# Splitting the first query load of an attention lead-in, with four fewer idle transposes

## The chip, the cores and the metric

The kernel runs on one NeuronCore of a Trainium2 chip. The metric is the device time of one execution in microseconds (us); the number compared is the median over runs.

## The reference

The computation is a thresholded attention followed by a two-layer MLP with a hard-swish gate. B = 8 batches, H = 8 heads, S = 576 tokens, D = 64, all float32.

```python
scores = (q @ k.T) / sqrt(D)
scores = where(scores >= max(scores) - tau, scores, -1e9)
attn = softmax(scores)                      # sum + 1e-9 in the denominator
x = (attn @ v) as [B*S, H*D]                # 4608 x 512
h = x @ w_in                                # 512 -> 2048
out = (h * clip(h + 3, 0, 6) / 6) @ w_out   # 2048 -> 512
```

## The kernel before

Heads are handled four at a time, a "quad" (16 quads in all, two per batch), and within a quad as two pairs of heads. A pair's queries and keys must stand with the head dimension on the partitions before their product can be formed, so each pair's blocks are transposed once: on TensorE (PE) for the first two batches, on VectorE (DVE) later. A quad gives nine "slots": eight of 128 queries by 576 keys for two heads, and one for the remaining 64 tokens of all four heads. The 144 slots run one after the other in an order written out by hand: in slot n the kernel computes the row maxima of slot n+1 (L302, DVE), mask and exponential (L309, L314, ScalarE, here ACT), normalisation (L322, GpSimd, here POOL), the scores of slot n+2 (L287, PE), and in the gaps the products with v and the MLP's matmuls.

The change is in the lead-in, the stretch ahead of slot 0. There is no scheduler: every engine executes its instructions in the order in which the program lists them, and a transfer starts in the order in which its queue's engine issues it. The names in it:

- `load_quad(0)` puts five load jobs in a list, and all are started at once: keys of pair 0 (`load_k(0)`, tile `km`, two transfers of 128 KB, one per head), queries of pair 0 (`load_q(0)`, tile `nq`, two of 128 KB), the last 64 tokens of keys and queries (`rest`, tiles `kr` and `nq`, four of 32 KB), and keys and queries of pair 1. All are issued by SyncE (SP), except the queries of pair 0, which ACT issues. A partition's piece of any of these loads is runs of 64 floats, 256 bytes each. For queries, tile t holds tokens 128t to 128t + 127; for keys a partition holds four successive tokens.
- `warm_up(17)` (L185) issues 17 transposes of a 128x128 float32 identity into a PSUM bank that nobody reads. They depend on the identity alone.
- Then the real transposes, in this order on PE: four of the keys (L232), `warm_up(4)`, the first 128 tokens of the queries (L456), the rest of the keys (L457), three more query tiles (L459), three more idle transposes (L461), and the scores of slots 0 and 1 (L287).
- The evictions from PSUM: ACT copies the main keys (L222) and half of the rest of the keys (L465); DVE copies the first queries (L464), the other half of the rest of the keys (L466), and the other queries (L467).
- After that, `warm_up(8)` in slot 0 and `warm_up(6)` in slots 0 to 7 put further idle transposes behind the scores.

```python
    load_quad(0)
    start(loads, 5)
    ...
    warm_up(17)
    ...
    evict = transpose_k(0)
    warm_up(4)
    nc.tensor.transpose(lead[:, 0, 0:P], q_main[:, 0, 0:2, :], identf[:])   # L456
    nc.tensor.transpose(lead[:, 1, 0:P], nat[0][2][:], identf[:])           # L457
    for t in range(1, 4):
        nc.tensor.transpose(q_rows[:, t * P:(t + 1) * P], q_main[:, t, 0:2, :], identf[:])  # L459
```

Transfers signal one of eight semaphores in turn; a ninth transfer uses the first one again and waits for its earlier transfer.

Of the kernel before, what the change touches and what calls it, by code (L numbers as in the profile page):

```python
# [15 lines left out]
P = 128  # L16
# [4 lines left out]
def kernel(  # L21
# [10 lines left out]
    nc = tc.nc  # L32
# [8 lines left out]
    NB = 2  # L41
# [40 lines left out]
    def load_quad(quad):  # L82
        b, g = divmod(quad, 2)
        nat[quad] = (nat_pool.tile([P, 1152], F32, tag="nq", name="nq"),
                     nat_pool.tile([P, 4, 4, D], F32, tag="km", name="km"),
                     nat_pool.tile([P, 2 * D], F32, tag="kr", name="kr"))
        nq, km, kr = nat[quad]

        def main(dst, src, h, order, by=nc.sync):
            by.dma_start(out=dst[:, :, h, :], in_=src[b, 4 * g + h, 0:512, :].rearrange(order, t=4))  # L90

        def blocks_q(n, a, j):
            c = 32 * (2 * a + j)
            nc.sync.dma_start(out=nq[c:c + 32, n * S:(n + 1) * S].rearrange("p (k d) -> p k d", d=32),
                              in_=q[b, 4 * g + 2 * n + a, :, 32 * j:32 * j + 32].rearrange("(k r) d -> r k d", r=32))

        def blocks_k(n, a, j):
            c = 32 * (2 * a + j)
            nc.sync.dma_start(
                out=km[c:c + 32].rearrange("p t h d -> p (t h d)")[:, n * 512:(n + 1) * 512].rearrange(  # L100
                    "p (t m d) -> p t m d", t=4, d=32),
                in_=k[b, 4 * g + 2 * n + a, 0:512, 32 * j:32 * j + 32].rearrange("(m r t) d -> r t m d", r=32, t=4))

        def load_k(n):
            if b < NB:
                for a in range(2):
                    main(km, k, 2 * n + a, "(p t) d -> p t d")
            else:
                for a in range(2):
                    for j in range(2):  # L110
                        blocks_k(n, a, j)

        def load_q(n):
            if b < NB:
                for a in range(2):
                    main(nq[:, 0:1024].rearrange("p (t h d) -> p t h d", h=4, t=4), q, 2 * n + a, "(t p) d -> p t d",
                         by=nc.scalar if quad == n == 0 else nc.sync)
            else:
                for a in range(2):
                    for j in range(2):  # L120
                        blocks_q(n, a, j)

        def rest():
            for dst, src in ((kr[:], k), (nq[:, 1024:1152], q))[0:2 if b < NB else 1]:
                for n in range(2):
                    (nc.sync if b < NB else nc.gpsimd).dma_start(out=dst[64 * n:64 * n + 64, :].rearrange("p (h d) -> p h d", h=2),
                                      in_=src[b, 4 * g + 2 * n:4 * g + 2 * n + 2, 512:S, :].rearrange("h p d -> p h d"))

        def both():
            rest()  # L130
            load_k(1)

        if b < NB:
            loads.extend((lambda: load_k(0), lambda: load_q(0), rest, lambda: load_k(1), lambda: load_q(1)))
        else:
            loads.extend((lambda: load_q(0), lambda: load_k(0), lambda: load_q(1), both))
# [46 lines left out]
    def warm_up(count):  # L183
        for _ in range(count):
            nc.tensor.transpose(ps[:, HB, 0:P], identf[:], identf[:])  # L185

    warm_up(17)
    identb = singles.tile([P, P], BF16)
    nc.vector.tensor_copy(out=identb[:], in_=identf[:])
    three = singles.tile([P, 1], F32)  # L190
# [181 lines left out]
    def mm1(item, hb=HB):  # L372
        b, ni, c0 = item
        if c0 is None:
            for ki in range(KI):
                nc.tensor.matmul(ps[:, hb, :], xR[b // 2][:, ki, :], w_in_sb[:, ki, ni * P:ni * P + 512],  # L376
                                 start=(ki == 0), stop=(ki == KI - 1))
        else:
            for n in range(2):
                for ki in range(KI):  # L380
                    nc.tensor.matmul(ps[:, hb, n * 256:(n + 1) * 256], w_in_sb[:, ki, (ni + n) * P:(ni + n + 1) * P],  # L381
                                     xT[b][:, ki, c0:c0 + 256], start=(ki == 0), stop=(ki == KI - 1))
        return ps[:, hb, :]
# [134 lines left out]
    for n, sl in enumerate(queue):  # L518
        quad, slot = sl.quad, sl.slot
        b, g = divmod(quad, 2)  # L520
# [25 lines left out]
        if todo1:  # L546
            item, then = todo1.pop(0)
            h = mm1(item, OB if n > N1 and n % 2 and not pieces else HB)
# [149 lines left out]
```

## Time and profile before

| | |
|---|---|
| median of 4 runs | 522.12 us (521.65 to 523.26) |
| profiled execution, its time | 521.65 us |
| its span, first to last instruction | 519.9 us |
| PE busy | 502.9 us, 97% |
| DVE, ACT, POOL busy | 442.3, 451.9, 299.3 us |
| lead-in, up to the first scores matmul | 7.03 us |

Times inside the profile count from the span's start. "L232" is line 232 of the kernel before. In the timeline a row gives the start, the length, the engine, the line and operation, the tiles written and read, and how many instructions were merged; square brackets give the idle time before it and what ended it. "SPq" and "ACTq" rows are transfers being issued, "PEld" is the weight load of a matmul. A PE record is longer than the distance to the next one because matmuls are pipelined, so rates are read from distances or from a stretch divided by its count.

### The profile page before, as it was taken

The numbers are of one execution on the slowest core, as the hardware profiler recorded it, in microseconds if no ns is written. First come the engines' busy times: TensorE is split into PE (matmuls) and PEld (weight loads), VectorE is DVE, ScalarE is ACT, GpSimd is POOL, SyncE is SP. The second block draws the span as 40 slices with busy tenths as digits, with TensorE's granted clock in tenths as the row PEclk, the third lists the DMA queues.
The fourth block names the chain that finished last, engine by engine and source line by source line (L and its number), as shares of the span: only waits on it lengthen the run. The fifth ranks groups of instructions, "written<-read, shape, count | busy, mean of one in ns | idle before, by whom it ended". The sixth has DMA issues, their size and how long they took to land.

```text
span 519.9 us, 12068 instructions
## 1 busy us (share of the span) xinstructions
PE 502.9 (97%) x4089; PEld 321.1 (62%) x4145; DVE 442.3 (85%) x1124; ACT 451.9 (87%) x980; POOL 299.3 (58%) x538
## 2 busy tenths in 40 slices
PE   8999999999999999999999999999999999999997
PEld 6765556666665666666655666666655666667463
DVE  3788888998999999999999999999999999878151
ACT  3999979999999999999999999999999999995060
POOL 1788869756676666657566656657566755551000
PEclk9999999999999999999999999999999999999999
DMA  5899999989999899999999999999999996564222
GB/s 131 125 173 156 153 152 136 203 140 177 166 175 165 157 174 154 193 160 180 163 168 179 173 175 160 178 161 178 161 172 162 177 170 113 112 113 70 83 61 61
DMA packets 314094, 78.77 MB, mean 152 GB/s; under 512 B 296624, under 2 KB 309168, under 8 KB 314032
## 3 DMA queue, kind: packets, MB, share of 16 engines
q1 hardware_dynamic: 294464, 67.90, 77.3%
q0 software_dynamic: 18368, 9.71, 15.0%
q8 instruction: 32, 0.52, 0.4%
q10 hardware_dynamic: 1200, 0.39, 0.3%
q14 instruction: 30, 0.25, 0.2%
HBM read 36.70 MB, written 9.44 MB: 89 GB/s over the span
## 4 chain that ended last, share of the span: by engine, by line
PE 77%; ACT 3%; DVE 2%; issue 2%; DMA 1%; POOL 0%; POOLq 0%; DVEq 0%
PE ps L287 24%; PE ps L415 23%; PE ps L381 19%; PE ps L346 6%; PE ps L376 2%; ACT s L309 1%; PE ps L349 1%; ACT s L314 1%; DMA pR<-pn 1%; ACT r L389 1%; DMA g<-go 1%; DVE s L302 1%; DVE g L404 1%; POOL pn L322 0%; PE ps L257 0%
## 5 line engine op out<-in xcount | busy, mean ns | idle before, releaser
L322 POOL TENSOR_SCALAR pn<-s,rinv 128x576 bf16<-128x576 f32 x288 | 210.6, 743 | 19.5 <-issue 4.4
L302 DVE TENSOR_SCALAR_CACHE_REDUCE s<-ps 128x576 f32<-128x576 f32 x288 | 205.0, 748 | 17.6 <-PE ps L287 9.0
L309 ACT ACTIVATE s<-s,bias 128x576 f32<-128x576 f32 x288 | 205.9, 763 | 6.0 <-POOL bias L305 5.7
L314 ACT ACTIVATE s<-s 128x576 f32<-128x576 f32 x288 | 192.5, 671 | 0.3
L287 PE MATMUL ps<-kT,qT 64*128 64x384 f32 (+7 forms) x1280 | 174.0, 419 | 4.7 <-DVE s L302 3.8
L287 PEld LDWEIGHTS ps<-kT,qT 64*128 64x128 f32 (+1 forms) x1280 | 103.6, 175 | 59.3 <-issue 15.8
L381 PE MATMUL ps<-xT,w_in_sb 128*128 128x256 bf16 x1024 | 130.8, 273 | 1.3 <-DVE g L404 0.7
L415 PE MATMUL ps<-w_out_sb,g 128*128 128x512 bf16 x524 | 123.4, 379 | 2.8 <-issue 0.2
L381 PEld LDWEIGHTS <-w_in_sb 128*128 128x128 bf16 x1024 | 95.5, 98 | 41.0 <-issue 22.1
L305 POOL TENSOR_SCALAR bias<-m 128x2 f32<-128x2 f32 x144 | 26.9, 187 | 154.1 <-DVE rinv L317 135.6
L404 DVE SCALAR_TENSOR_TENSOR g<-r,ps 128x512 bf16<-128x512 f32 x128 | 87.6, 686 | 9.5 <-ACT r L389 5.5
L415 PEld LDWEIGHTS <-g 128*128 128x128 bf16 x576 | 56.3, 98 | 56.7
L389 ACT ACTIVATE r<-ps,three 128x512 f32<-128x512 f32 x81 | 55.4, 687 | 28.9 <-PE ps L381 21.3
L314 ACT ACTIVATION_READ_ACCUMULATOR s<-s 128x1 f32 x288 | 54.5, 189 | 0.0
L391 DVE TENSOR_SCALAR r<-ps 128x512 f32<-128x512 f32 x63 | 42.9, 680 | 0.0
L346 PE MATMUL ps<-pT,vm 128*64 128x256 bf16 (+1 forms) x480 | 39.1, 285 | 0.0
L346 PEld LDWEIGHTS <-vm 128*64 128x64 bf16 x736 | 27.2, 110 | 16.6 <-issue 15.4
L357 DVE CAST xT<-ps 128x256 bf16<-128x256 f32 (+1 forms) x60 | 26.2, 437 | 12.8 <-PE ps L349 12.8
L423 DVE TENSOR_SCALAR osb<-ps 128x512 f32<-128x512 f32 x31 | 20.9, 673 | 13.3 <-PE ps L415 13.3
L302 DVE DVE_READ_ACCUMULATOR s<-ps 128x1 f32 x288 | 23.8, 83 | 0.0
L317 DVE RECIPROCAL rinv<-rsum 128x2 f32<-128x2 f32 x144 | 23.0, 160 | 0.6 <-ACT s L314 0.6
L143 POOL DMA_DIRECT2D vm<-in_v_dram x28 | 21.4, 766 | 0.7 <-issue 0.7
(57 smaller groups left out, 259.1 us busy)
## 6 DMA issues: line engine op xcount, KB each, us to landing
out_dram<-osb SPq DMA_DIRECT2D x31, 256.0 KB, 2.8
nq<-in_q_dram SPq DMA_DIRECT2D x96, 72.0 KB, 3.4
km<-in_k_dram SPq DMA_DIRECT2D x96, 64.0 KB, 3.1
vm<-in_v_dram POOLq DMA_DIRECT2D x24, 128.0 KB, 4.0
km<-in_k_dram SPq DMA_DIRECT2D x16, 128.0 KB, 3.7
w_in_sb<-in_moe_w_in_dram POOLq DMA_DIRECT2D x16, 128.0 KB, 3.7
w_out_sb<-in_moe_w_out_dram POOLq DMA_DIRECT2D x16, 128.0 KB, 4.8
pT<-pn SPq DMA_TRANSPOSE x117, 4.0
```

Source lines behind the costliest of these rows:

```text
L287: nc.tensor.matmul(ps_flat[rows, c0:c0 + w], qT_of(pair)[a * 64:(a + 1) * 64, q0:q0 + rows.stop - rows.start], kT_of(pair)[a * 64:(a + 1) ...
L302: nc.vector.tensor_scalar(out=sl.s[:, i, :], in0=ps_flat[:, c0:c0 + S], scalar1=1.0, scalar2=None, op0=Alu.mult, op1=Alu.max, accum_out=sl ...
L305: nc.gpsimd.tensor_scalar(out=sl.bias[:], in0=sl.m[:], scalar1=-scale, scalar2=tau, op0=Alu.mult, op1=Alu.add)
L309: nc.scalar.activation(out=s, in_=s, func=Act.Prelu, bias=sl.bias[:, i:i + 1], scale=scale, alpha=REJECT)
L314: nc.scalar.activation(out=s, in_=s, func=Act.Exp, accum_out=sl.rsum[:, i:i + 1])
L322: nc.gpsimd.tensor_scalar(out=pn[:, i, :], in0=sl.s[:, i, :], scalar1=sl.rinv[:, i:i + 1], scalar2=1.0, op0=Alu.mult, op1=Alu.mult)
L346: nc.tensor.matmul(pb[a * 64:(a + 1) * 64, :], vm[:, 2 * hp + a, c * D:(c + 1) * D], pT[:, 5 * a + c, cols], start=(c == 0), stop=False)
L381: nc.tensor.matmul(ps[:, hb, n * 256:(n + 1) * 256], w_in_sb[:, ki, (ni + n) * P:(ni + n + 1) * P], xT[b][:, ki, c0:c0 + 256], start=(ki = ...
L389: nc.scalar.activation(out=r, in_=hps, func=Act.Relu, bias=three[:])
L391: nc.vector.tensor_scalar(out=r, in0=hps, scalar1=3.0, scalar2=0.0, op0=Alu.add, op1=Alu.max)
L404: nc.vector.scalar_tensor_tensor(out=out, in0=r, scalar=6.0, in1=hps, op0=Alu.min, op1=Alu.mult)
L415: nc.tensor.matmul(o_ps[0], gbuf[:, ni, mt * P:(mt + 1) * P], w_out_sb[:, ni, :], start=(ni == 0), stop=(ni == NI - 1))
```

## The change

The first pair's queries, two transfers of 128 KB on ACT's queue before, become three on the same queue: the first 128 tokens of both heads (64 KB), and then tokens 128 to 511 of each head (96 KB each). The transpose of the first query tile then depends on the 64 KB alone, that of the three others on the two larger transfers. The idle transposes ahead of the keys go from 17 to 13. Nothing else differs: on PE, DVE, ACT, POOL and SP the order of all other instructions stays as it was.

```diff
         def load_q(n):
-            if b < NB:
+            if quad == n == 0:
+                rows = nq[:, 0:1024].rearrange("p (t h d) -> p t h d", h=4, t=4)
+                nc.scalar.dma_start(out=rows[:, 0, 0:2, :], in_=q[0, 0:2, 0:P, :].rearrange("h p d -> p h d"))
                 for a in range(2):
-                    main(nq[:, 0:1024].rearrange("p (t h d) -> p t h d", h=4, t=4), q, 2 * n + a, "(t p) d -> p t d",
-                         by=nc.scalar if quad == n == 0 else nc.sync)
+                    nc.scalar.dma_start(out=rows[:, 1:4, a, :], in_=q[0, a, P:512, :].rearrange("(t p) d -> p t d", t=3))
+            elif b < NB:
+                for a in range(2):
+                    main(nq[:, 0:1024].rearrange("p (t h d) -> p t h d", h=4, t=4), q, 2 * n + a, "(t p) d -> p t d")
...
-    warm_up(17)
+    warm_up(13)
```

More of the change, by code (lines that the diff above doesn't have):

```diff
@@ L87, in load_quad, with main @@
         nq, km, kr = nat[quad]
-        def main(dst, src, h, order, by=nc.sync):
-            by.dma_start(out=dst[:, :, h, :], in_=src[b, 4 * g + h, 0:512, :].rearrange(order, t=4))
+        def main(dst, src, h, order):
+            nc.sync.dma_start(out=dst[:, :, h, :], in_=src[b, 4 * g + h, 0:512, :].rearrange(order, t=4))
         def blocks_q(n, a, j):
```

## The prediction

> **What bounds the kernel now.** I read the page's busy shares first, then the waits of PE over the whole span, then the timeline of the first microseconds.
>
> ```profile
> PE 502.9 (97%) x4089; PEld 321.1 (62%) x4145; DVE 442.3 (85%) x1124; ACT 451.9 (87%) x980; POOL 299.3 (58%) x538
> ...
> PE ps L287 <- DVE s L302: 3.8, 6, 1.0
> PE ps L337 <- POOL pn L322: 2.2, 8, 0.3
> ...
> PE ps L346 <- DMA pR<-pn: 0.5, 1, 0.5
> ```
>
> PE bounds the kernel. All its recorded waits together are a few us (each row: waited for, us in total, times, longest), and the only one on a transfer is 0.5 us, long after the lead-in. Behind the first scores, work follows work: no load has a wait of its own that could swallow an earlier start. So what the lead-in gains or loses arrives at the end about one for one, and the question is only when the first scores start. The timeline of the lead-in:
>
> ```profile
> 0.74 0.99 ACTq L90 DMA_DIRECT2D nq<-in_q_dram  x2
> 0.74 1.39 SPq L90 DMA_DIRECT2D km<-in_k_dram  x2
> ...
> 1.37 3.89 PE L185 MATMUL ps<-identf 128*128 128x128 f32 x17 [1.37 <-POOL identf masks.py:199]
> ...
> 2.18 1.30 SPq L126 DMA_DIRECT2D kr<-in_k_dram  x2
> ...
> 5.16 0.63 PE L232 MATMUL ps<-identf,km 128*128 128x128 f32 x4
> ...
> 5.83 0.59 ACT L222 COPY kT<-ps 128x512 f32<-128x512 f32 x1 [2.79 <-PE ps L232]
> ...
> 6.17 0.27 PE L457 MATMUL ps<-identf,kr 128*128 128x128 f32 x1
> ...
> 6.48 0.26 ACT L465 COPY kT<-ps 64x128 f32<-64x128 f32 x1
> ...
> 6.77 0.29 DVE L466 COPY kT<-ps 64x128 f32<-64x128 f32 x1
> 7.03 1.33 PE L287 MATMUL ps<-kT,qT 64*128 64x384 f32 x8
> ```
>
> From the right: scores (7.03) follow L466 (6.77), which follows L465 (6.48), which follows PE's L457 (6.17), which stands in PE's order behind the keys' transposes (5.16). So all hangs on the start at 5.16. Two things end there together. The view of `km` for the second key transfer alone (issued 1.52) gives its landing:
>
> ```profile
> DMA to landing us min/median/max: 3.5/3.5/3.5
> ```
>
> 1.52 + 3.5 = 5.02. And the 17 idle transposes hold PE until about 5.05. The third thing is the rate of PE (stretch, length, PE busy and count):
>
> ```profile
> 1.37:5.16 3.79, 3.79 (x17) 3.51 (x18) 0.21 (x3) 1.28 (x1) 0.00 (x0) 1.00 0.73 163
> 5.16:7.03 1.87, 1.87 (x17) 1.70 (x16) 0.55 (x2) 0.84 (x2) 0.00 (x0) 1.00 0.40 92
> ```
>
> 17 transposes take 3.79 us in the first stretch and 1.87 us in the second: 0.22 and 0.11 us each, same shape, same type. PE runs at half rate until just about 5.16 and at full rate after. The clock column shows 1.00 in both, so the step is seen in the durations alone. Starts in narrower timelines (2.27, 2.70, 3.13, two apart) give 0.213 for the slow spacing.
>
> **The change part by part.**
>
> *Fewer bytes ahead of the second key transfer.* In the transfer view of 1.8 to 4.2 us the engines are full at a mean of 227 GB/s, 250 in most slices; 128 KB takes 0.52 us. Before, the second key transfer had 128 (q) + 128 (k) + 128 (q) = 384 KB before it. Now 64 + 128 + 96 = 288 KB were issued ahead of it, since ACT's issues took 0.43 and 0.53 us and the third would be issued from about 1.75 to 2.25, while SP issues its second from 1.52 to 2.14. 96 KB less is 0.39 us: landing at 5.02 - 0.39 = 4.63. Bounds: the six `km` loads of the first 9 us have a smallest issue-to-landing of 2.7 us, so no earlier than 4.2; if the last 96 KB of queries share the engines turn by turn, nothing is gained and it lands at 5.02. I take 4.63.
>
> *Four idle transposes fewer.* 4 x 0.213 = 0.85 us: PE is free at 5.05 - 0.85 = 4.20, so this alone removes PE's own hold, and the keys decide. PE now stands still from 4.20 to about 4.73 (4.63 and 0.1 us from landing to the first matmul), a gap the profile before doesn't have.
>
> *Transposes of the keys.* They begin at 4.73 instead of 5.16, 0.43 us earlier. But if PE's rate steps up at the same time as before (5.16), the first two run at 0.213, and two at 0.109: the fourth starts at 4.73 + 2 x 0.213 + 0.109 = 5.27, against 5.16 + 0.36 = 5.52 (first spacing 0.14 as recorded). Gain 0.25 us. From there everything shifts alike: keys' copy 5.83 -> 5.58, L457 6.17 -> 5.92, L465 6.23, L466 6.52, scores 6.78.
>
> *What must be there for that.* The rest of the keys (issued 2.87, 2.5 us to landing: 5.4) is needed at 5.92, cover 0.5 us; it is also the floor: L457 can't start before about 5.4, so the lead-in can't gain over 0.77 us. The first query tile waits for 64 KB that is first on its queue, landed by about 3 us. The other query tiles (L459, needed at 6.03) wait for the last of the same 512 KB in all, which landed by 5.02 before: cover 1 us. If that cover were gone, PE would stop ahead of L459, and the scores queue behind it.
>
> *One transfer more on ACT, and moved semaphores.* About 0.5 us of issuing before ACT's table load (1.76 to 3.04): it moves to about 2.3 to 3.6, hidden by the wait for the keys (2.79 us before L222). With nine transfers ahead of pair 1 where there were eight, SP's second `rest` load of queries and all later ones wait for a neighbouring semaphore; the earlier users of those landed more than 1 us before each issue, so I cost it at nothing; the bound is one issue (0.6 us) on loads that are used only at 14 us.
>
> *The clock.* The trace of before has no gap in this stretch, so it can't show what one does. Row first: PE had done nothing but transposes from 1.37 to 5.16 and its rate doubled after 3.8 us. [...] Bounds: 0 and, if the next pause of PE (0.77 us before 9.12 waiting for DVE) spoils that too, 3 us. The value I take is 0: the stretch around the gap is still 85% busy (0.5 of 3.8 us idle), nearer to a full stretch than to an idle one. That is a choice, not something that a row shows.
>
> **Sum.** -0.25 us against the profiled execution (521.65): 521.40. Its time stands 0.47 below the median of the four runs, so against the median 522.12 - 0.25 = 521.9.
>
> **Rivals.**
>
> *1. The clock steps up late (slower).* Place: PE between 4.2 and 8.5. The nine transposes up to L457 take 9 x 0.213 = 1.92 instead of 1.0: L457 at 6.65 (+0.48). The other seven take 1.5: scores start at 8.15 (+1.1). They run slow till 8.5, which costs another 0.2: +1.3 us, so 523.4. With a second missed step, +3: 525. For it: [...] that the lead-in's other waits are all filled with idle work. Against it: a gap of 0.5 us is short, and the DVE-bound pause of 0.77 us before 9.12 did not slow the matmuls after it. It decides if the gap delays the step by over 2 us; below that the earlier keys pay for it.
>
> *2. The keys don't land earlier (no change).* Queues may be served in turn, so that the removed bytes come back from the third transfer. Then PE waits from 4.2 to 5.02 and starts at 5.1 as before: 522.1. For it: the landings of ACT's two loads (2.4 and 3.2 us after issue) and of SP's (3.0 and 3.5) interleave. Against: each queue was served in large pieces.
>
> *3. A larger gain.* Keys at 4.2, and a step of the rate no later: -0.5 to the floor of -0.77, 521.4 to 521.6. Beyond 1 us faster, only other runs' luck remains.
>
> **How the numbers follow.** Measurements of this kernel spread so that 0.2%, 1.04 us, is about what can be told from no change. Likeliest case 0.40, rival 2 0.12, rival 3 0.10, rival 1 0.38 (of which 0.03 ends under 1.04 us). Of the first three, 0.12 could come out over 1.04 us faster, with the spread of the runs (521.65 to 523.26) on top. That gives faster 0.12, same 0.53, slower 0.35. Range: 521.2 (floor of -0.77 and a little of the spread) to 523.8 (rival 1 at one late step and 0.4 of spread), leaving out the double miss. The likeliest case's own range is 521.3 to 522.3.
>
> **What would show it.** Right: second `km` transfer landing near 4.6, L185 with 13 ending near 4.2, L232 starting near 4.7 with two long and two short records, scores at 6.8, the transposes from L456 on at 0.109 spacing. Rival 1: transposes L456 to L461 at 0.213 spacing and scores beyond 8. Rival 2: L232 at 5.1. I am wrong altogether if the scores start earlier and the end doesn't follow.

## The result, and the profile after

The changed kernel takes 524.13 us (median of 39 runs, 522.37 to 527.10) against 522.15 for the kernel before (60 runs, 521.21 to 524.50). The ratio is 1.0033, 95% interval 1.0026 to 1.0041: about 1.7 us slower (the two medians lie 2.0 us apart). The forecast was 521.9, with a range up to 523.8; the kernel came out above it. The times of the changed kernel fall into two groups: 11 of the 39 runs lie between 522.37 and 523.22, and 24 above 523.85. Of the 60 runs before, one is above 523.85.

The profiled execution took 524.98 us, with a span of 523.2. In the kernels with the split load the line numbers are four higher (L189 is the old L185). The timeline of the lead-in (start, length, engine, line and operation; idle time before it in brackets):

```profile
1.37 3.03 PE L189 MATMUL ps<-identf 128*128 128x128 f32 x13 [1.37 <-POOL identf masks.py:199]
...
5.37 1.09 PE L236 MATMUL ps<-identf,km 128*128 128x128 f32 x4 [0.97 <-DMA km<-in_k_dram]
...
7.32 0.42 PE L461 MATMUL ps<-identf,kr 128*128 128x128 f32 x1
...
8.06 0.29 DVE L470 COPY kT<-ps 64x128 f32<-64x128 f32 x1 [0.21 <-ACT kT L469]
8.17 0.85 PE L465 MATMUL ps<-identf 128*128 128x128 f32 x3
...
8.95 1.96 PE L291 MATMUL ps<-kT,qT 64*128 64x384 f32 x8
...
10.94 0.76 DVE L306 TENSOR_SCALAR_CACHE_REDUCE s<-ps 128x576 f32<-128x576 f32 x1 [1.33 <-PE ps L291]
```

The keys start at 5.37, 0.2 us later than before and not 0.4 earlier. The second key transfer, issued at 1.52, landed at 5.24, against 5.03 before:

```profile
DMA to landing us min/median/max: 3.7/3.7/3.7
```

The transfer view of 1.8 to 5.4 us, in 40 slices of 0.09 us, shows a part of the reason. Busy share of the DMA engines in tenths, the kernel before and then the changed one:

```profile
DMA  1388999988999999999999999973354110146400
DMA  2598435402799999999999999999997532254310
```

Behind the short first query transfer the engines were half busy or less from about 2.2 to 2.7 us. From 1.8 to 4.2 us they moved 202 GB/s on average where they had moved 227, which is some 60 KB less and by estimate 0.26 of the 0.39 us that the forecast gained. The rest is not resolved; the third query transfer landed at 5.41, so it moved at least in part beside the keys and not behind them.

From the start of the keys' transposes to the scores PE needs 3.6 us where it needed 1.9: all its transposes are 0.21 us apart. The trace's record of the full clock begins at 10.44 us here, against 5.18 in the profile before; the spacing halves there. The first reduction starts at 10.94 instead of 8.30, 2.64 us late. The last of the 288 reductions is 2.63 us late (466.65 against 464.02): nothing in 455 us swallowed any of it.

But the span is 3.3 us longer, so 0.7 us more is lost after the last reduction. The waits of PE show where (us in total, times, longest):

```profile
PE ps L350 <- DMA pR<-pn: 1.3, 1, 1.3
PE ps L236 <- DMA km<-in_k_dram: 1.0, 1, 1.0
```

The wait for `km` is the new gap. The wait for `pR`, a transposing transfer near 480 us, was 0.5 us before. Nothing in the diff touches it.

### The profile page after: what moved, and what is told of

Read it like the earlier page. It is cut to its first block, busy times and chain, and to the rows that moved or that the text cites. A ratio compares the mean times of both kernels' runs of the same rounds, so it can differ in the third digit from the quotient of the medians.

```text
span 523.2 us, 12061 instructions
## 1 busy us (share of the span) xinstructions
PE 504.5 (96%) x4085; PEld 321.9 (62%) x4141; DVE 442.4 (85%) x1124; ACT 451.9 (86%) x980; POOL 299.3 (57%) x538
## 4 chain that ended last, share of the span: by engine, by line
PE 77%; ACT 3%; DVE 2%; issue 2%; DMA 2%; POOL 0%; POOLq 0%; DVEq 0%
PE ps L291 24%; PE ps L419 23%; PE ps L385 19%; PE ps L350 6%; PE ps L380 2%; ACT s L313 1%; PE ps L353 1%; ACT s L318 1%; DMA pR<-pn 1%; ACT r L393 1%; DMA g<-go 1%; DVE s L306 1%; DVE g L408 1%; POOL pn L326 0%; PE ps L261 0%
```

## The experiments

"Ratio" is to the kernel before, timed on the same chip in the same rounds, with its 95% interval. "Step" is where the trace's record of the full clock begins.

**The two halves of the change, each alone.** First the split loads with all 17 idle transposes (`e1`), then the whole loads with 13 (`e2`).

```diff
 # e1: the changed kernel
-    warm_up(13)
+    warm_up(17)
 # e2: the kernel before
-    warm_up(17)
+    warm_up(13)
```

> The split query load with the 17 idle transposes kept. Theory A (the gap in PE's work spoils the step to the full rate): the keys land near 5.2 as in the changed kernel, the transposes end near 5.05, so PE stands still for some 0.3 us instead of 1.0; the rate steps up between 5 and 8 us in most runs and the time is within 0.2% of before (522 to 523). Theory B (the transfers cost the time: the keys or the rest of the keys land later): as slow as the changed kernel, 524.

> The whole query loads of before with 13 idle transposes instead of 17. Theory A: the keys land at 5.0, the transposes end at 4.2 to 4.4, PE stands still for about 0.8 us, and the time is nearly that of the changed kernel: 523.5 to 524. Theory B: PE's gap costs nothing, the keys set the start as before: 522.1.

`e1`: 522.41 us, ratio 1.0008 (1.0000 to 1.0017). `e2`: 523.72 us, ratio 1.0030 (1.0016 to 1.0044). The missing transposes carry the loss; the split alone costs at most 0.9 us by its interval. The timeline of `e2`:

```profile
1.37 3.04 PE L185 MATMUL ps<-identf 128*128 128x128 f32 x13 [1.37 <-POOL identf masks.py:199]
5.19 1.09 PE L232 MATMUL ps<-identf,km 128*128 128x128 f32 x4 [0.79 <-DMA km<-in_k_dram]
...
8.77 1.86 PE L287 MATMUL ps<-kT,qT 64*128 64x384 f32 x8
```

The same picture as the changed kernel, without its transfers: a gap of 0.79 us, a step at 10.05, scores at 8.77. In `e1` the second key transfer landed at 4.95 (5.03 before), so the keys were hardly earlier for the split.

**The gap filled.** `e3` is the changed kernel with `warm_up(21)`.

> The split load with 21 idle transposes, four more than before: they end near 5.9, so that the real ones start some 0.5 to 0.7 us later than the keys allow, but no gap is left. Theory A: near before, 522 to 523, and faster than the changed kernel though its PE has eight transposes more to do ahead of the keys. If only the time of the first real transpose counts, it is slower than the changed kernel by 0.3 us or more: 524.5.

522.10 us, ratio 1.0001 (0.9992 to 1.0011). Eight transposes more than in the changed kernel, and by the two ratios some 1.7 us faster. In its profile the step came at 4.50:

```profile
1.37 4.02 PE L189 MATMUL ps<-identf 128*128 128x128 f32 x21 [1.37 <-POOL identf masks.py:199]
5.22 0.60 PE L236 MATMUL ps<-identf,km 128*128 128x128 f32 x4
...
7.06 1.23 PE L291 MATMUL ps<-kT,qT 64*128 64x384 f32 x7
```

The 21 transposes ended near 5.2 and not near 5.9, since those after 4.50 took half the time (all 21 took 3.85 us up to the first of the keys, where 17 took 3.79 in the profile before).

**As few transposes, but no gap.** `e4` is the kernel before with 13 idle transposes that start later:

```diff
...
+    held = singles.tile([P, P], F32)
+    for _ in range(3):
+        nc.vector.memset(held[:], 0.0)
+    nc.vector.tensor_copy(out=held[:], in_=identf[:])
-    warm_up(17)
+    warm_up(13, held)        # transposes of held instead of identf
```

> The whole loads of before and 13 idle transposes, but on a copy of the identity that DVE makes only after three memsets, so that they start near 2.2 instead of 1.37 and end near 5.0, at the keys' landing, with no gap. Theory A, in which unbroken work counts: the step comes about 0.8 us later than before on average, half of which is lost: +0.4 us, 522.5, clearly under the 13 transposes with a gap. A theory in which the number of idle transposes counts, and not the gap: as slow as 13 with the gap, 523.5 to 524.

522.57 us, ratio 1.0011 (1.0003 to 1.0018), as expected. They started at 2.46, ran into the keys with no gap, and the step came at 6.68:

```profile
2.46 3.04 PE L185 MATMUL ps<-held 128*128 128x128 f32 x13 [2.46 <-DVE held L190]
...
5.29 1.06 PE L236 MATMUL ps<-identf,km 128*128 128x128 f32 x4
```

With 13 transposes both times, the gap makes the difference between 1.0011 and 1.0030.

**Smaller and larger gaps.** The kernel before with `warm_up(15)` (`e5`) and `warm_up(1)` (`e6`).

> The whole query loads of before with 15 idle transposes: a gap of about 0.4 us before the keys, half of that with 13. Theory A with a threshold on the share of busy time (the step came after a stretch of 3.4 us that was 92% busy in one profile, and did not come after stretches of 72 and 77%): 0.4 of 3.4 us is 88% busy. If the threshold is below that, the time is that of before, 522.1; if it is above, it is near the 13: 523.5. If each missing transpose costs alike, half of the loss: 522.9.

> The whole loads of before with one idle transpose instead of 17, so that PE stands still from about 1.8 to 5.1. Theory A: the work counts from the keys on, and the step comes at 8 to 12 us: 524.5 to 525.5, little worse than with 13 and a gap in its worse runs, but with none of the runs near 522. If each missing transpose costs what the four cost (0.4 us each), it is slower than before by 6 us: 528.

`e5`: 521.66 us, ratio 1.0006 (0.9990 to 1.0021), not told from before; its profile has a gap of 0.26 us and a step at 4.76. `e6`: 523.24 us, ratio 1.0027 (1.0014 to 1.0039), with a step at 10.54. One transpose is no worse than thirteen and a gap, which refutes a price per transpose. It was even 1 us better than theory A said; a part of the reason comes below (PE did not wait for `pR` at all).

**The changed kernel, two more profiles.**

> The changed kernel once more, one look. In its first profile the rate stepped up at 10.4 us and the first reduction began at 10.94. If the place of the step against PE's start is drawn anew in each execution (theory A), this profile may show another: with a step at 5 to 8 us, scores near 7 to 8 and a time near 522.5; with a late one the same picture as before. If the late step belongs to the kernel in every execution, it is at 10.4 again.

> The changed kernel a third time, as the second: a step between 8 and 12 us with a time over 524, or between 5 and 8 us with a time near 522.5, and nothing between that does not fit the first reduction's start.

522.04 and 522.81 us, with steps at 4.70 and 4.14. The step is drawn anew in each execution. In `e8` the lead-in went as the forecast had it (4.73 and 6.78 there):

```profile
4.91 0.63 PE L236 MATMUL ps<-identf,km 128*128 128x128 f32 x4 [0.51 <-DMA km<-in_k_dram]
...
6.78 1.33 PE L291 MATMUL ps<-kT,qT 64*128 64x384 f32 x8
```

The match at 6.78 is luck in part: the keys came 0.18 us later than forecast and the step 0.46 us earlier. The scores are 0.25 us ahead of before, and the execution was still slower than the profiled one of before (521.65), since it too waited 1.3 us for `pR`.

What decides the step? In all 19 profiles the record of the full clock lasts 512.00 or 515.41 us (515.41 in the profile before, 512.00 in the first one of the changed kernel). The two lie 3.41 us apart and are 150 and 151 times 3.4133 us, so by inference the record begins and ends on a grid of that spacing. The stretches of the grid ahead of the step can then be counted back from it. PE's busy time in them, from the windows view (stretch, length, PE busy): the stretch that ended 3.41 us before the step of the changed kernel's first profile and the one of `e2`, neither followed by a step, then that of `e9`, which ended with one. (The 1.00 in these rows is no reading of the clock: the trace has no clock record before the step.)

```profile
3.61:7.02 3.41, 2.44 (x12) 2.06 (x11) 0.00 (x0) 0.53 (x1) 0.00 (x0) 1.00 0.61 133
```

```profile
3.22:6.64 3.42, 2.63 (x13) 2.26 (x12) 0.00 (x0) 0.32 (x1) 0.00 (x0) 1.00 0.56 124
```

```profile
0.73:4.14 3.41, 2.77 (x13) 2.63 (x13) 0.71 (x4) 1.28 (x1) 0.49 (x2) 1.00 0.61 138
```

72% and 77% busy: no step. 81% busy: a step. The other profiles agree: counted so, every stretch that ended with a step was at least 81% busy (89% in `e8`, 92% in `e3`), and every earlier one at most 77%. If PE's busy time is what counts, which stays an inference, the bar lies between 77% and 81% in these profiles, and a gap of 0.8 to 1.0 us that fell into one stretch cost a whole stretch more (steps at 10.44 and, in `e2`, 10.05). That would account for the two groups of runs. An estimate from the first profile: with its gap from 4.40 to 5.37 us and a bar of 80%, the first stretch that PE's work can fill passes only if it ends between 4.10 and 5.08 us, which is 0.98 of 3.41 us or 29% of the executions; 11 of the 39 runs, 28%, are in the faster group. That it fits so closely is partly luck, since the gap varies from 0.51 to 1.18 us.

**The keys moved instead.** If the keys were early, 13 transposes would leave no gap. `e7` is the changed kernel with the second head's keys issued first on ACT's queue; `e10` is the same again; `e11` does it with whole query loads.

```diff
...
-                    main(km, k, 2 * n + a, "(p t) d -> p t d")
+                    main(km, k, 2 * n + a, "(p t) d -> p t d",
+                         by=nc.scalar if quad == n == 0 and a else nc.sync)
```

> The changed kernel (split queries, 13 idle transposes) with one more move: the second head's keys are issued first on ACT's queue, ahead of the queries, instead of second on SP's. If the idea of the change is right and only the arrival of the keys was misjudged, both keys land near 3.9, the 13 transposes end with no gap, the keys' transposes start near 4.2, 0.95 us earlier than before, and the first query tile and the rest of the keys are there in time; the time is 0.5 to 0.9 us below before: 521.2 to 521.6. If the transfers behind the keys then come late (rest of the keys after 5.3), it is the same as before: 522.

> The two-queue keys with the split queries again, for a second profile and a second median: the first profile had the keys 1 us earlier and the first reduction where the best profile of before has it with a step that came 1 us later, but its last transposing transfer (pR) landed 0.6 us later than in the profile of before and PE waited for it. If that is chance per execution, the pR wait differs now and the median is at or below before (521.5 to 522.2 against some 522); if it belongs to this order of transfers, PE again waits over 1 us for pR and the median is 0.5 us above before.

> The keys on two queues, ahead of the whole query loads of before, and 13 idle transposes: the split undone, only the keys moved. The keys land near 3.9 and there is no gap. If the split brings something once the keys are early, this is slower than the split with two queues by up to 0.3 us (the first query tile lands with its whole 128 KB near 4.5, still ahead of its use at 5.7); if not, they are the same. By theory A both are free of the loss of the changed kernel: 521.3 to 522.3.

`e7`: 522.30 us, ratio 1.0015 (1.0008 to 1.0021). `e10`: 522.51, 1.0010 (1.0000 to 1.0021). `e11`: 522.54, 1.0009 (1.0002 to 1.0016). The keys did land in time (3.88 in `e7`), and PE started on them at 4.19 with no gap. Yet the kernels were slower than before. All three profiles have a wait of 1.1 to 1.3 us for `pR`. So that wait is no chance, and a second cause must be in the change. `e4` has it too (1.1 us), and `e2` (1.0), so the two differ in the gap and not in this wait.

**A fetch of PE's instructions.** The transfer view around the last `pR` transfer, in 40 slices of 0.14 us: busy share of the DMA engines, then GB/s. The kernel before (474.0 to 479.5, issue at 474.27):

```profile
DMA  0000000060299999900000089998000000000000
GB/s 0 0 0 0 0 0 0 0 119 0 58 201 207 203 192 73 11 4 7 9 9 9 9 168 289 290 292 174 0 0 0 0 0 0 0 0 0 0 0 0
...
q8 instruction: 1, 0.02, 1.5%
...
pR<-pn SPq DMA_TRANSPOSE x1, 4.0
```

The changed kernel (476.5 to 482.0, issue at 476.90):

```profile
DMA  0000000000029999999999000000000092000000
GB/s 0 0 0 0 0 0 0 0 0 0 0 60 220 218 216 201 203 218 331 171 132 34 0 0 0 0 7 7 9 9 11 11 200 66 0 0 0 0 0 0
...
pR<-pn SPq DMA_TRANSPOSE x1, 4.9
```

Beside the transfer a 16 KB packet of queue q8 (instructions) runs for 1.1 to 1.3 us on one DMA engine: the single 119 GB/s slice before, the 331 GB/s slice after. It starts 0.86 us after the issue of `pR` before, 2.10 us after it in the changed kernel, in the middle of the transfer. The traces do not name the engine that q8 serves. It carried 32 packets in each profile, and between two of them PE started some 250 matmuls and weight loads on average (252 in the profile before, 212 to 289 at a time). That suggests that each packet is a fetch of PE's next instructions. Then fewer instructions on PE must shift the place of every later fetch. Two kernels test it: `e12` gives the changed kernel four idle transposes in a pause of slot 2; `e13` takes four from the kernel before in slot 7.

```diff
 # e12
+        if n == 2:
+            warm_up(4)
         if n <= N1:
             scores(n + 2)
 # e13
         if n < 8:
-            warm_up(6)
+            warm_up(2 if n == 7 else 6)
```

> The changed kernel with four idle transposes more in slot 2, where PE stands still for 0.9 us ahead of the scores (waiting for DVE's copy of the keys), so that PE has as many instructions as before but the same gap ahead of the first keys. Theory F (a fetch of PE's instructions falls into the last pR transfer): the fetch is back at about 0.9 us after that transfer's issue, PE's wait for pR back at 0.5 us or less, and the median falls by 0.5 to 0.7 us, to about 523.3, with the late clock steps still in it. If the pR wait has nothing to do with the instruction count, the wait stays at 1.1 to 1.3 us and the median at 524.

> The kernel before, with its 17 idle transposes and the whole loads, and four idle transposes fewer in slot 7, at 38 us: lead-in and clock as before. Theory F: the fetch falls about 2 us after the issue of the last pR transfer, PE waits 1.1 us or more for it, and the median is 0.5 to 0.7 us above before, 522.6. If the clock is the only loss: as before, 522.0.

The packet moved as the theory says: to 0.82 us after the issue in `e12` and to 1.98 in `e13`. That it brings PE's instructions stays an inference; "fetch" stands for it below. The waits followed, `e12` first:

```profile
PE ps L350 <- DMA pR<-pn: 0.4, 1, 0.4
```

```profile
PE ps L346 <- DMA pR<-pn: 1.0, 1, 1.0
```

All 19 profiles fall into three sorts. In six the packet starts 0.8 to 1.2 us after the issue of `pR`, which lands 3.7 to 4.2 us after it (`e14` has no record of it), and PE waits 0.2 to 0.6 us. In nine, all with four transposes fewer than before, it starts 1.9 to 2.1 us after the issue, `pR` lands after 4.5 to 4.9, and PE waits 1.0 to 1.3. In the four with 12 or more fewer it starts at 2.6 to 3.2, `pR` lands after 3.2 to 3.4 where the landing is recorded, and no wait is listed.

The times say less. `e12`: 524.02 us, ratio 1.0026 (1.0017 to 1.0036); nine of 22 runs lie between 521.3 and 523.1, with a median of 522.3 against 522.6 for the lower group of the changed kernel, but the median of all is among the slower runs and missed the 523.3. `e13`: 522.02, ratio 1.0007 (0.9999 to 1.0016), less than expected; the four transposes taken away in slot 7 gave back 0.44 us on the spot in its profile (the reductions went from 0.80 us late to 0.36 there, against the profile before).

**Both causes out of the way.** `e14` is `e7` with four idle transposes in slot 2. `e15` is `e7` without those of slots 6 and 7, `e16` the kernel before without them, `e17` is `e7` without those of slots 4 to 7.

```diff
 # e15 and e16 (e17: n < 4)
-        if n < 8:
+        if n < 6:
             warm_up(6)
```

> Both keys issued first on two queues, split queries, 13 idle transposes with no gap, and four more in slot 2's pause, so that the fetch is where it was before. Theory F with theory A: the lead-in is 0.3 to 0.9 us shorter than before at the same clock step, and the pR wait no longer takes it back: 0.3 to 0.6 us faster than before, 521.5. Without F: as in the two looks at two queues, 0.5 above before.

> As the two-queue kernel with 13, but without the idle transposes of slots 6 and 7: 12 fewer on PE, as in the kernel with one idle transpose, whose fetch came 2.7 us after the issue of the last pR transfer and whose PE did not wait for it at all. Theory F: no pR wait, 0.5 us less than even before; with the earlier keys 0.7 to 1.0 us faster than before: 521.1. If idle work in slots 6 and 7 is needed for the clock: slower than 522.

> The kernel before with its own lead-in (17 idle transposes, whole loads), but without the 12 idle transposes of slots 6 and 7. In the two-queue kernel without them the later reductions came 0.6 us earlier against the first one, and the pR wait was gone (another 0.5 us). If both belong to the 12 transposes, this is 1.1 us faster than before, 520.9, and the earlier keys are worth the remaining 0.5 to 0.7 us; if the earlier keys carry the gain, it is as before.

> The two-queue kernel without the idle transposes of slots 4 to 7: 24 fewer. If idle work in these slots only takes PE's time once the clock is up, another 0.5 us is gained and the fetch stays behind the last pR transfer: 519.6. If the clock needs it (a step that comes late or falls back between 18 and 40 us), it is slower than with 12 fewer: 520.5 or more.

`e14`: 522.28 us, ratio 1.0002 (0.9994 to 1.0009), the wait for `pR` back at 0.5, no measurable gain: the earlier keys alone do not show in the median. `e15`: 520.09 us, ratio 0.9965 (0.9954 to 0.9977). `e16`: 520.50 us, ratio 0.9970 (0.9959 to 0.9981). These beat both kernels, and most of the gain belongs to the 12 transposes of slots 6 and 7, not to the keys. It has two parts: in `e16` the reductions gain 0.6 us across these slots, and the stretch after the last reduction is 0.7 us shorter, since the fetch starts 2.7 us after the issue of `pR` and PE's waits have no row for `pR` any more. In the profile of `e17` the last reduction is 1.39 us ahead of before, another 0.8 us against `e15`; but 0.5 of these were there at the first reduction, with a step at 5.02 against 6.03, and only 0.26 came in slots 4 and 5. The end then lost it: 521.87 us, ratio 0.9995 (0.9986 to 1.0003). A q8 packet fell into a late `g` transfer (issued at 495.90), on which DVE's gate waits, and PE waits for that:

```profile
PE ps L385 <- DVE go L408: 2.2, 1, 2.2
```

```profile
q8 instruction: 1, 0.02, 1.2%
...
g<-go SPq DMA_TRANSPOSE x1, 4.7
```

In `e16` that transfer had no q8 packet beside it, landed in 3.1 us, and the wait was 0.6. Not every late transfer has such a packet: the profiles of `e9`, `e11` and `e12` lose 0.3 to 1.0 us in mid-run, at waits of PE for a `pT` transfer; a q8 packet stood beside the late one in `e9`, none beside those in `e11` and `e12`. That stays open.

## Why the prediction was wrong

- *"What the lead-in gains or loses arrives at the end about one for one"*: right, 2.64 us at the first reduction and 2.63 at the last. It was taken too far: the end has a transfer wait of its own (the 0.5 us that the prediction showed and set aside as long after the lead-in), and the edit reached that wait by another way, through the place of the fetch.
- *Keys at 4.63*: the term was mis-sized. The second key transfer landed at 5.24, 4.78 and 5.38 in the three profiles of the changed kernel, against 5.03 before. Rival 2, queues served so that nothing is gained, comes nearer; the choice of the mean rate over 96 KB did not hold, since the engines ran part empty near 2.5 us.
- *PE free at 4.20, with a gap of 0.5*: by the spacing PE was free as computed, though the last transpose's record ends at 4.40. Counted from that end the gap was 0.51, 0.97 and 1.18 us, since the keys landed late. (The prediction's 17 transposes in the second stretch are 16, as one had begun before it; the spacing of 0.109 stands.)
- *The clock, "the value I take is 0"*: this is the step that failed. Rival 1 had the late step, and 1.3 us for it, with the step at 8.5: the keys' 4.73 and once more the 3.8 us that came ahead of the step in the profile before. That PE's work counts afresh after a gap was an estimate of the author's; no run shows it. The step came at 10.44, and the first profile lost 2.6. The reason given for 0, that the stretch is still 85% busy, rested on a gap of 0.5 us, and so on the keys at 4.63; with gaps of 0.8 to 1.0 us the stretches were 72 to 77% busy and the step was missed. The forecast could have seen it without the keys: its own rival 2 has PE waiting from 4.2 to 5.02 and still counts nothing for the clock. `e2`, with the keys at 5.06, is that case: the first reduction in its profile is 2.4 us late. In the two profiles with an early step nothing was lost to the clock. It is a lottery with a price, not one price.
- *"PE had done nothing but transposes from 1.37 to 5.16 and its rate doubled after 3.8 us"*: right that these transposes bring the step. `e3` stepped up at 4.50 after nothing but idle transposes. The 3.8 us were those of one execution: steps came from 2.8 us after PE's start on (at 4.14 in `e9`, with PE from 1.37).
- *The semaphores and the extra ACT issue, costed at nothing*: no wait on them is seen. The ninth transfer, issued at 4.17, asks for the semaphore of the first (issued at 0.74), which had landed at 2.6.
- *Missing altogether*: that four transposes fewer on PE move a fetch into a transfer 475 us later. It adds 0.5 to 0.7 us after the last reduction in every profile of the changed kernel. By estimate from these profiles some 0.6 of the 1.7 us belong to it and the remaining 1.1 to the clock. The times do not settle this to better than some tenths: `e12` and `e13` moved the fetch, but the intervals of their ratios are 0.9 to 1.0 us wide.

## What to carry to other kernels

In this kernel, idle work ahead of the step of PE's clock should reach the first real work with little or no gap (0.26 us cost nothing that shows in `e5`, 0.8 us did in `e2`); take some of it away only with the arrival of the data seen in the profile, and profile several executions, since the step was drawn anew in each (10.44, 4.70 and 4.14 us in the three of the changed kernel). Idle work after the clock is up can be plain cost: 12 transposes fewer there gave 1.6 us in `e16`, more than anything done to the loads, but only about 0.6 us of it is their own time; most of the rest came from where the fetch happened to fall, and `e17` lost that part again by the same accident. Before explaining a wait far from an edit by the edit's data, look for an instruction packet beside the transfer that is late.

## What the runs showed of the hardware

The 16 KB packets of q8 beside the `pR` transfers and the late `g` took 0.9 to 1.3 us on a DMA engine (0.88 to 1.83 us for all those of the two main profiles), and the `pR` transfer landed 3.2 to 4.9 us after its issue, depending on where the packet fell (latest, at 4.5 to 4.9 us, with the packet 1.9 to 2.1 us after the issue). Four transposes more or fewer on PE moved it: from 2.10 us after the issue to 0.82 in `e12`, from 0.86 to 1.98 in `e13`. The number of instructions on PE is thus a hidden parameter of this tuned kernel. The record of the full clock lasted 512.00 or 515.41 us, and the 3.41 us that ended with its start were at least 81% busy on PE. And one idle transpose ahead of the keys came out no worse than thirteen with a gap (1.0027 and 1.0030), though `e6` was spared the wait for `pR` that `e2` had.
